# A third buffer for x, one mask tile, and a new order of VectorE's work in a routing attention followed by an MLP

## The chip, the cores and the metric

The kernel runs on one core of one Trainium2 chip. The metric is the device time of one execution in microseconds, as the median of a few runs. The core has five engines with a queue of instructions each, and each queue runs in order: TensorE (PE in the profile, its weight loads PEld), VectorE (DVE), ScalarE (ACT), GpSimd (POOL) and SyncE (SP). Engines wait for each other through semaphores. All transfers between DRAM and SBUF run on 16 shared DMA engines. In this kernel SyncE issues most of them, and GpSimd the small ones and those that add to their target.

## The reference

There are two parts. The first is attention over 4 batches, 8 heads, 768 positions and a head size of 64, in which a query sees only the keys that were routed to the same one of 16 clusters. The second is an MLP with a layer norm and a residual on the 512 features of the joined heads.

```python
q_assign = argmax(q_n @ c_n.T)            # q_n, k_n, c_n: rows over their norms
k_assign = argmax(k_n @ c_n.T)
mask = q_assign[:, None] == k_assign[None, :]
scores = where(mask, q @ k.T / sqrt(D), -1e9)
attn = exp(scores - max) / (sum(exp(scores - max)) + 1e-9)
x = (attn @ v), heads side by side        # (4, 768, 512)
xn = (x - mean) / sqrt(var + 1e-6) * g_ln
out = x + relu(xn @ w_ch1) @ w_ch2        # 512 -> 2048 -> 512
```

The weights of the MLP come as float64 and are turned to float32 on the chip.

## The kernel before

**Pairs and slots.** The attention handles two heads at a time. There are 16 such pairs n (batch and head pair), and each is worked in two slots, one for each half of the 768 queries. A slot has six steps, one for each block of 128 keys. A step i is `scores(i)` and later `weigh(i)`.

- `scores` (L390) makes a 128 x 768 block of scores in PSUM: two matmuls that add the mask and two of keys by queries (L406). ScalarE then takes the exponential into a tile e (L401; eight buffers). PSUM has three buffers for scores, so TensorE can be three steps ahead of ScalarE.
- `weigh` (L411) multiplies e with v into the accumulator a_ps (L418). On VectorE it adds the six e tiles of a slot to a running sum es for the denominators (L432, L435). After the last step ScalarE copies the accumulator into the pair's x tile (L444). x has two buffers, `xs[n]` (L439).

**Preparing the next pair.** For pair n + 1, k is turned (`prep_transpose`, L273), on VectorE in 32 x 32 blocks when it was loaded in the layout for that (`blocks`, L78; line 280). q is turned in that way for pair 1 and from pair 7 on, and on TensorE with a copy by ScalarE for pairs 2 to 6 (L285, L290). `prep_sims` (L305, matmul L312) makes the similarities to the centroids, `prep_turn` (L324) turns them, and `prep_route` (L333) finds the best cluster and writes one-hots on VectorE (L337, L339). `prep_onehot` (L349) turns the one-hots, and ScalarE shades them into two tiles, m and mask, which are the mask's factors (L375). There are two of each.

**Finishing a pair.** `finish(n, part)` (L448) has four parts. Part 0 sums es over the keys by a matmul (den_ps, L455), copies it (L463) and sends the rows to DRAM and back in another layout (flat, rdens: L465, L466). Part 1 takes reciprocals on VectorE (L470), sends them to DRAM (row, L472) and loads them broadcast over the partitions into rb (L480, one buffer). Part 2 multiplies x with rb in place of rb (L487) and stores it. This frees the x buffer. Part 3 turns the product into y (L496) and stores that too. Parts 2 and 3 of pair n run two pairs later.

**Other work between.** For the MLP, weights are converted in chunks: six VectorE instructions (`split_weight`, `join_weight`, L245 to L265) and a transfer by GpSimd that adds to the target (L268). That is two chunks a pair up to pair 6 and one afterwards (`convert`, L622). The layer norm of the first batch (`norm_rows`, `norm_stats`, `norm_stat_rows`, `norm_apply`), sums of its x (`x_sum`) and of the first weights (`w1_sums`) are hung onto pairs 6 to 15 by `put` (L598).

**What sets the order.** The attention is in two blocks `manual_schedule` (L628, L666). Inside a block TensorE, VectorE and ScalarE take instructions in the order in which the program lists them. SyncE's order in the second block is set by a scheduler that builds the program, and so is how the two blocks interlock at their seam, which lies between the first three steps' scores with the turning of k and q of pair 1, and the loop over the slots. In the loop (L667) a slot of pair n lists, before the change: its scores; in slot 0 `finish(n - 1, 0)` and the similarities of n + 1; in slot 1 the one-hots and masks of n + 1; then the conversion; then the weighing with VectorE's sums; then in slot 0 `finish(n - 2, 2)` and `(.., 3)`, the turning of the similarities and the routing of n + 1, and in slot 1 `finish(n - 1, 1)` and the turning of k and q of n + 2; last, the jobs that `put` has hung there. VectorE's part of that, for slot 0 of a middle pair:

```
conversion (6), sums (5), scaling L487, turning y L496, best L337, one-hots L339
```

and for slot 1:

```
conversion (6), sums (5), reciprocals L470, turning k (and q) L280
```

**After the attention** come two layers for each of the four batches, both as Strassen-like products of seven with sums on VectorE and ScalarE (`first_layer`, L791; `second_layer`, L879). The first batch's layers need nothing of the last pair, but the matmul of the last denominators (`finish(15, 0)`, L925) stands ahead of it in TensorE's order.

Of the kernel before, what the change touches and what calls it, by code (L numbers as in the profile page):

```python
# [8 lines left out]
F32 = mybir.dt.float32  # L9
BF16 = mybir.dt.bfloat16  # L10
# [9 lines left out]
def kernel(  # L20
# [11 lines left out]
    nc = tc.nc  # L32
    B, H, S, D = q.shape
    NCL = centroids.shape[1]
    DM, FF = moe_w_ch1.shape
    P = 128
# [19 lines left out]
    def pool(name, bufs, **kw):  # L56
        return stage.enter_context(tc.tile_pool(name=name, bufs=bufs, **kw))

    loads = pool("loads", 1)
    heads = pool("heads", 2)  # L60
# [4 lines left out]
    last = pool("last", 1)  # L65
# [4 lines left out]
    def ps(name, dt=F32, n=512):  # L70
        return pools["t"].tile([P, n], dt, tag="t", name=name)

    pairs = [(b, pr) for b in range(B) for pr in range(NPAIR)]
# [4 lines left out]
    blocks = {  # L78
        (n, name) for n in range(1, len(pairs)) for name in ("qk" if n == 1 or n >= TWICE else "k")
    }  # L80
# [63 lines left out]

    mask = [heads.tile([P, S], BF16, name=f"mask_{i}", bufs=1) for i in range(2)]
    for m in mask:
        nc.gpsimd.memset(m, 0.0)
    hits = const.tile([P, B * NPAIR], F32, name="hits")  # L150
    far = const.tile([P, 2], F32, name="far")
    for rows, bias, scale in ((slice(0, D), 0.0, 1.0), (slice(D, P), -FAR, FAR)):
# [118 lines left out]
    prepared = {n: {} for n in range(len(pairs))}  # L271

    def prep_transpose(n, side, halves=range(NHALF)):  # L273
        src = loaded[n]["qk"[side]]
        if 0 in halves:
            prepared[n][side] = heads.tile([P, S], F32, tag=f"t{side}", name=f"t{side}")
        t_sb = prepared[n][side]
        if (n, "qk"[side]) in blocks:
            if 0 in halves:
                nc.vector.transpose(t_sb, src)  # L280
            return
        if n:
            t = ps_s.tile([P, 2, 512], F32, tag="s", name="qk_ps")
            for c in range(NT):
                nc.tensor.transpose(  # L285
                    t[:, c // TH, c % TH * P : (c % TH + 1) * P],
                    src[:, c, :, :].rearrange("p h d -> p (h d)"),
                    ident,
                )
            nc.scalar.copy(t_sb.rearrange("p (g c) -> p g c", g=NHALF), t[:, :, :HC])  # L290
            return
        for g in halves:
            t = ps_s.tile([P, 2, 512], F32, tag="s", name="qk_ps")[:, 0]
            for c in range(TH):
                nc.tensor.transpose(
                    t[:, c * P : (c + 1) * P],
                    src[:, g * TH + c, :, :].rearrange("p h d -> p (h d)"),
                    ident,
                )
            if side == 0 or g == 1:  # L300
                nc.scalar.copy(t_sb[:, g * HC : (g + 1) * HC], t[:, :HC])
            else:
                nc.vector.tensor_copy(t_sb[:, g * HC : (g + 1) * HC], t[:, :HC])
# [45 lines left out]
    def prep_onehot(n):  # L349
        t = ps("oh_ps", BF16, 1024)  # L350
        for g in range(NHALF):
            for c in range(TH):
                o = (g * TH + c) * P
                nc.tensor.transpose(
                    t[:, o : o + P],
                    onehot[:, c, g, :, :, :].rearrange("p s j d -> p (s j d)"),
                    identb,
                )

        m = heads.tile([P, S], BF16, tag="m", name="m")  # L360
        shade(n, m, t[:, :S], slice(0, P))
        z = mask[n % 2]
        prepared[n]["oh"] = t
        prepared[n]["m"] = [(z[:D], m[:D]), (m[D:], z[D:])]

    def prep_mask(n, j):
        t, z = prepared[n]["oh"], mask[n % 2]
        src, dst = ((D, 0), (Q, D + Q))[j]
        src, dst = slice(src, src + NCL), slice(dst, dst + NCL)
        shade(n, z[dst], t[src, :S], src)  # L370

    def shade(n, out, src, rows):
        add, factor = far[rows, 0:1], far[rows, 1:2]
        if n:
            nc.scalar.activation(out, src, AF.Identity, bias=add, scale=factor)  # L375
        else:
            nc.vector.tensor_scalar(out, src, factor, add, op0=ALU.mult, op1=ALU.add)  # L377
# [6 lines left out]
    xs = {}  # L384
# [26 lines left out]
    def weigh(i):  # L411
        n, g, c = steps[i]
        e = soft[i]
        if c == 0:
            accs[n, g] = ps_a.tile([P, 512], F32, tag="a", name="a_ps")
        acc = accs[n, g]
        for j in range(2):
            nc.tensor.matmul(  # L418
                acc[j * D : (j + 1) * D, :HC],
                loaded[n]["v"][:, j, c, :],  # L420
                e[:, j, :],
                start=(c == 0),
                stop=(c == NT - 1),
            )

        if c == 1:
            if n + 1 < len(pairs):
                es = last.tile([P, 2, HC], F32, tag="es", name="es", bufs=3)
            else:
                es = xpool.tile([P, 2, HC], F32, tag="row", name="es", bufs=2)  # L430
            sums[n, g] = es
            nc.vector.tensor_tensor(es, soft.pop(i - 1), soft.pop(i), ALU.add)  # L432
        elif c > 1:
            es = sums[n, g]
            nc.vector.tensor_tensor(es, es, soft.pop(i), ALU.add)  # L435
        if c == NT - 1:
            if g == 0:
                if n + 1 < len(pairs):
                    xs[n] = last.tile([P, S], F32, tag="x", name="x", bufs=2)  # L439
                else:  # L440

                    late["all"] = xpool.tile([P, 3, S], F32, tag="sums", name="late", bufs=2)
                    xs[n] = late["all"][:, 0]
            nc.scalar.copy(xs[n][:, g * HC : (g + 1) * HC], accs.pop((n, g))[:, :HC])  # L444
# [153 lines left out]
    def put(n, slot, f, *args):  # L598
        extra.setdefault((n, slot), []).append(lambda: f(*args))
# [1 line left out]
    put(6, 0, norm_load, 0)  # L601
    put(6, 1, rows_load, 0, 0)
    for t in range(NT):
        put(7 + t // 2, t % 2, norm_rows, 0, t)
    put(9, 1, norm_stats, 0)
    put(10, "between", norm_stat_rows, 0)
    for i in range(2):
        for c in range(NDC):
            put(10 + 2 * i + c // 2, 1 if i == 0 else c % 2, norm_apply, 0, i, c)
    put(14, 0, x_sum, 0, 1)  # L610
    put(14, 1, x_sum, 0, 2)
    put(15, 1, w1_sums, 0, 0, (0, 1))

# [50 lines left out]
    with tc.manual_schedule(engines=order | {mybir.EngineType.Pool}):  # L666
        for u in range(len(pairs) * slots):  # L667
            n, slot = divmod(u, slots)
            nxt = n + 1 < len(pairs)
            own = range(GROUP * u, GROUP * (u + 1))  # L670
            if slot == 0 and not nxt:
                finish(n - 1, 0)
            for i in own:
                if i >= AHEAD:
                    scores(i)
            if slot == 0:
                if n and nxt:
                    finish(n - 1, 0)
                if nxt:
                    prep_sims(n + 1)  # L680
            elif nxt:
                prep_onehot(n + 1)
                prep_mask(n + 1, 0)
                prep_mask(n + 1, 1)
                if n + 2 < len(pairs) and (n + 2, "q") not in blocks:
                    prep_transpose(n + 2, 0)
                    load(n + 3, "q")
            for job in extra.pop((n, "between"), ()) if slot else ():
                job()
            if (n, slot) in convert:  # L690
                m = convert[n, slot]
                split_weight(m)
                join_weight(m)
                load_weight(m + 1)
            for i in own:
                weigh(i)
            if slot == 0:
                load(n + 1, "v")
                if n > 1:
                    finish(n - 2, 2)  # L700
                    finish(n - 2, 3)
                if nxt:
                    prep_turn(n + 1)
                    prep_route(n + 1)
                else:
                    finish(n - 1, 1)
            elif not nxt:
                for part in (2, 3):
                    finish(n - 1, part)
            else:  # L710
                if n:
                    finish(n - 1, 1)
                if n + 2 < len(pairs):
                    for side in (1, 0):
                        if (n + 2, "qk"[side]) in blocks:
                            prep_transpose(n + 2, side)
                            load(n + 3, "qk"[side])
            for job in extra.pop((n, slot), ()):
                job()

# [471 lines left out]
```

## Time and profile before

The time is 952.88 us, the median of three runs (950.92 to 953.88). The profiled execution spans 951.0 us.

| engine | busy us | share | instructions |
|---|---|---|---|
| TensorE | 922.8 | 97% | 4664 |
| VectorE | 618.1 | 65% | 1106 |
| ScalarE | 346.7 | 36% | 549 |
| GpSimd | 79.2 | 8% | 147 |

By stage, from the busy time in windows, in us and as the share of DMA engines in use:

| window | TensorE | VectorE | ScalarE | DMA |
|---|---|---|---|---|
| 60 to 100 | 38.3 of 40 | 35.2 | 26.2 | 0.88 |
| 100 to 150 | 45.2 of 50 | 42.2 | 30.6 | 0.83 |
| 150 to 200 | 48.8 of 50 | 46.8 | 32.1 | 0.93 |
| 200 to 250 | 48.2 of 50 | 45.0 | 38.0 | 0.84 |
| 250 to 300 | 42.4 of 50 | 38.2 | 27.6 | 0.72 |
| 300 to 350 | 49.4 of 50 | 45.8 | 36.2 | 0.52 |
| 600 to 700 | 100.0 of 100 | 45.5 | 16.3 | 0.11 |

A line of a timeline reads: start in us, duration in us (of the group, if several are merged), engine, line of the kernel, operation, output <- inputs, shape, count, and in brackets how long the engine was idle before it and what ended that wait. In a line of groups the two numbers after the bar are busy us in all and mean ns of one. The attention ends at about 364 us, with the last denominators' matmul; after that the two layers run.

### The profile page before, as it was taken

The page shows a single profiled execution, that of the slowest core. Times are in us where ns is not written, and L with a number is a line of the kernel's source. Part 1 is how long each engine was busy: PE and PEld are TensorE (multiplying, and loading weights), DVE is VectorE, ACT ScalarE, POOL GpSimd, SP SyncE. Part 2 cuts the span into 40 slices and gives each one's busy share as a digit, 9 for nine tenths or more (in the row PEclk, how much of TensorE's full clock was granted, in tenths as well). Part 3 has the DMA queues.
Part 4 walks back from the last instruction along what each step waited for, and adds up shares of the span by engine and source line. Part 5 has one row for each costly group of instructions (what it writes and reads, how often), then busy time and mean ns, then how long its engine had stood idle before and what let it go on. Part 6 is the DMA issues. An engine that isn't in the chain of part 4 may idle for free.

```text
span 951.0 us, 12611 instructions
## 1 busy us (share of the span) xinstructions
PE 922.8 (97%) x4664; PEld 591.0 (62%) x4664; DVE 618.1 (65%) x1106; ACT 346.7 (36%) x549; POOL 79.2 (8%) x147
## 2 busy tenths in 40 slices
PE   8999989999969999999999999999999999999997
PEld 5444444444434445557887557887557887556886
DVE  5998889999599987798882446362436472344431
ACT  4776657677647663332001332001332000332000
POOL 2111112121111121110000000000000000000000
PEclk9999999999979999999999999999999999999999
DMA  7668888988758644564451002021002021000011
GB/s 152 155 153 190 189 181 177 203 179 179 158 117 153 154 94 117 137 140 141 136 158 39 0 1 78 22 95 40 1 0 69 32 84 50 1 1 6 29 45 36
DMA packets 179780, 92.48 MB, mean 97 GB/s; under 512 B 145792, under 2 KB 162288, under 8 KB 179712
## 3 DMA queue, kind: packets, MB, share of 16 engines
q1 hardware_dynamic: 170368, 76.20, 33.0%
q0 software_dynamic: 7744, 15.02, 7.8%
q8 instruction: 38, 0.62, 0.3%
q10 hardware_dynamic: 1600, 0.39, 0.2%
q14 instruction: 30, 0.25, 0.1%
HBM read 64.10 MB, written 19.10 MB: 87 GB/s over the span
## 4 chain that ended last, share of the span: by engine, by line
PE 81%; DVE 9%; DMA 5%; issue 2%; ACT 1%; SPq 1%; POOL 0%; DVEq 0%; ACTq 0%; POOLq 0%
PE x_ps L853 17%; PE x_ps L760 16%; PE s_ps L406 10%; PE z_ps L853 9%; PE a_ps L418 8%; PE z_ps L760 8%; PE y_ps L853 4%; PE y_ps L760 4%; DVE es L435 2%; DMA rb<-row 1%; DMA v_sb<-in_v_dram 1%; DMA row<-rdens 1%; DVE w L260 1%; DVE tb L265 1%; DVE ta L248 1%
## 5 line engine op out<-in xcount | busy, mean ns | idle before, releaser
L406 PE MATMUL s_ps<-t,t 64*128 64x384 f32 x768 | 158.8, 492 | 0.0
L401 ACT ACTIVATE e<-s_ps 128x768 f32<-128x768 f32 x192 | 150.7, 814 | 21.6 <-PE s_ps L406 20.7
L435 DVE TENSOR_TENSOR es<-es,e 128x768 f32<-128x768 f32 x128 | 122.7, 958 | 14.7 <-ACT e L401 1.7
L418 PE MATMUL a_ps<-e,v_sb 128*64 128x384 f32 x768 | 130.9, 490 | 0.0
L780 DVE TENSOR_TENSOR h<-z_ps,u 128x384 f32<-128x384 f32 x64 | 35.6, 556 | 94.0 <-PE z_ps L760 71.9
L418 PEld LDWEIGHTS a_ps<-e,v_sb 128*64 128x64 f32 x768 | 52.3, 137 | 70.0 <-issue 58.1
L406 PEld LDWEIGHTS s_ps<-t,t 64*128 64x128 f32 x768 | 69.9, 191 | 33.8 <-issue 32.9
L853 PE MATMUL x_ps<-w2t,h 128*128 128x256 f32 x384 | 84.5, 379 | 0.0
L788 ACT ACTIVATE h<-h 128x384 f32<-128x384 f32 x96 | 49.6, 522 | 87.5 <-DVE h L780 87.5
L406 PE MATMUL s_ps<-m,mask 64*128 64x384 bf16 x192 | 63.0, 329 | 17.6 <-ACT e L401 17.6
L853 PEld LDWEIGHTS x_ps<-w2t,h 128*128 128x128 f32 x384 | 72.7, 190 | 10.1
L406 PE MATMUL s_ps<-mask,m 64*128 64x384 bf16 x192 | 63.0, 330 | 0.4 <-DVE mask L377 0.4
L775 ACT COPY u<-x_ps 128x384 f32<-128x384 f32 x64 | 30.6, 478 | 78.1 <-PE x_ps L760 78.1
L864 DVE TENSOR_TENSOR o_sb<-x_ps,xb 128x256 f32<-128x256 f32 x48 | 20.2, 420 | 50.2 <-PE x_ps L853 50.2
L775 ACT COPY p<-x_ps 128x384 f32<-128x384 f32 x32 | 14.9, 467 | 98.0 <-PE x_ps L760 98.0
L760 PE MATMUL x_ps<-xt,ws 128*128 128x384 f32 x128 | 46.6, 487 | 0.8 <-DVE ws L593 0.8
L444 ACT COPY x<-a_ps 128x384 f32<-128x384 f32 x30 | 14.3, 478 | 89.9 <-DVE rb L487 63.6
L760 PE MATMUL x_ps<-xn,w 128*128 128x384 f32 x128 | 46.6, 487 | 0.0
L760 PE MATMUL x_ps<-xt,w 128*128 128x384 f32 x128 | 46.5, 486 | 0.0
L760 PE MATMUL y_ps<-xn,w 128*128 128x384 f32 x128 | 46.5, 486 | 0.0
L760 PE MATMUL z_ps<-xn,ws 128*128 128x384 f32 x128 | 46.5, 486 | 0.0
L760 PE MATMUL z_ps<-xt,ws 128*128 128x384 f32 x128 | 46.5, 486 | 0.0
(146 smaller groups left out, 1382.9 us busy)
## 6 DMA issues: line engine op xcount, KB each, us to landing
raw<-in_moe_w_ch_dram SPq DMA_DIRECT2D x32, 512.0 KB, 4.5
w<-tb POOLq DMA_DIRECT2D x32, 256.0 KB, 5.1
v_sb<-in_v_dram SPq DMA_DIRECT2D x32, 192.0 KB, 4.6
xn<-xT_d SPq DMA_DIRECT2D x16, 384.0 KB, 5.3
xr<-x_d SPq DMA_DIRECT2D x24, 256.0 KB, 2.9
xb<-x_d SPq DMA_DIRECT2D x48, 128.0 KB, 2.2
out_dram<-o_sb SPq DMA_DIRECT2D x48, 128.0 KB, 1.7
k_sb<-in_k_dram SPq DMA_DIRECT2D x62, 96.0 KB, 3.9
```

Of the source, the lines that this page charges most:

```text
L248: nc.vector.scalar_tensor_tensor(out=ta, in0=hi, scalar=0xC0000000, in1=ta, op0=ALU.bitwise_and, op1=ALU.bitwise_or)
L401: nc.scalar.activation(e, s[:, :, :HC], AF.Exp, scale=SCALE)
L406: nc.tensor.matmul(s[:, j, :HC], of_keys[:, keys], of_queries[:, cols], start=part == first, stop=part != first, skip_group_check=True,)
L418: nc.tensor.matmul(acc[j * D : (j + 1) * D, :HC], loaded[n]["v"][:, j, c, :], e[:, j, :], start=(c == 0), stop=(c == NT - 1),)
L435: nc.vector.tensor_tensor(es, es, soft.pop(i), ALU.add)
L444: nc.scalar.copy(xs[n][:, g * HC : (g + 1) * HC], accs.pop((n, g))[:, :HC])
L760: nc.tensor.matmul(bank[:, :HC], lhs[:, c, :], rhs[:, c, :], start=first and c == 0, stop=c == NDH - 1, skip_group_check=True,)
L775: nc.scalar.copy(t, bank[:, :HC])
L780: nc.vector.tensor_tensor(h, bank[:, :HC], other, ALU.add)
L788: nc.scalar.activation(h, h, AF.Relu)
L853: nc.tensor.matmul(bank[:, :MH], hidden[lhs + (c,)][:, tt * P : (tt + 1) * P], rhs[:, c, :], start=first and c == 0, stop=c == NFH - 1, sk ...
L864: nc.vector.tensor_tensor(o, bank[:, :MH], x, ALU.add)
```

## The change

x gets a third buffer. The scaling and the turning of y (parts 2 and 3 of pair n - 2) move from slot 0, behind the sums, to slot 1, ahead of the sums. The third buffer is what makes that possible, since x of a pair now lives longer; the move is meant to take the copy of a_ps out of the wait for the scaling. The turning of k and q for the next pair moves from the end of slot 1 to the head of the next slot 0, so that it is done one slot before its use, not two. The conversion of weights moves behind the sums of its slot, so that the sums come as soon as the exponentials are there. The rows of the layer norm, its two passes of `norm_apply` and the sums of x and w1 are hung onto later places, so that the rows of statistics that come back from DRAM have more time to land. m and the mask go down to one tile each, which makes room in SBUF for the third x.

VectorE's work is now, for slot 0 and slot 1 of a middle pair:

```
turning k (and q), sums, conversion, best, one-hots
scaling, turning y, sums, conversion, reciprocals
```

In the order of the built program TensorE and ScalarE have the same sequences as before. VectorE's first sums (pair 0, slot 0) now stand ahead of the turning of k and q of pair 1, which is written in the first block; before, they stood behind it.

```diff
--- before.py
+++ after.py
@@ -144,9 +144,8 @@
-    mask = [heads.tile([P, S], BF16, name=f"mask_{i}", bufs=1) for i in range(2)]
-    for m in mask:
-        nc.gpsimd.memset(m, 0.0)
+    mask = heads.tile([P, S], BF16, name="mask", bufs=1)
+    nc.gpsimd.memset(mask, 0.0)
     hits = const.tile([P, B * NPAIR], F32, name="hits")
     far = const.tile([P, 2], F32, name="far")
     for rows, bias, scale in ((slice(0, D), 0.0, 1.0), (slice(D, P), -FAR, FAR)):
@@ -357,14 +356,14 @@
                     identb,
                 )
-        m = heads.tile([P, S], BF16, tag="m", name="m")
+        m = heads.tile([P, S], BF16, tag="m", name="m", bufs=1)
         shade(n, m, t[:, :S], slice(0, P))
-        z = mask[n % 2]
+        z = mask
         prepared[n]["oh"] = t
         prepared[n]["m"] = [(z[:D], m[:D]), (m[D:], z[D:])]
     def prep_mask(n, j):
-        t, z = prepared[n]["oh"], mask[n % 2]
+        t, z = prepared[n]["oh"], mask
         src, dst = ((D, 0), (Q, D + Q))[j]
         src, dst = slice(src, src + NCL), slice(dst, dst + NCL)
         shade(n, z[dst], t[src, :S], src)
@@ -436,7 +435,7 @@
         if c == NT - 1:
             if g == 0:
                 if n + 1 < len(pairs):
-                    xs[n] = last.tile([P, S], F32, tag="x", name="x", bufs=2)
+                    xs[n] = last.tile([P, S], F32, tag="x", name="x", bufs=3)
                 else:
                     late["all"] = xpool.tile([P, 3, S], F32, tag="sums", name="late", bufs=2)
@@ -601,15 +600,15 @@
     put(6, 0, norm_load, 0)
     put(6, 1, rows_load, 0, 0)
     for t in range(NT):
-        put(7 + t // 2, t % 2, norm_rows, 0, t)
+        put(7 + t // 2, 1, norm_rows, 0, t)
     put(9, 1, norm_stats, 0)
     put(10, "between", norm_stat_rows, 0)
     for i in range(2):
         for c in range(NDC):
-            put(10 + 2 * i + c // 2, 1 if i == 0 else c % 2, norm_apply, 0, i, c)
-    put(14, 0, x_sum, 0, 1)
-    put(14, 1, x_sum, 0, 2)
-    put(15, 1, w1_sums, 0, 0, (0, 1))
+            put(11 + 2 * i + c // 2, 1, norm_apply, 0, i, c)
+    put(15, 0, x_sum, 0, 1)
+    put(15, 0, x_sum, 0, 2)
+    put(15, 0, w1_sums, 0, 0, (0, 1))
@@ -670,6 +669,11 @@
             own = range(GROUP * u, GROUP * (u + 1))
             if slot == 0 and not nxt:
                 finish(n - 1, 0)
+            if slot == 0 and n and nxt:
+                for side in (1, 0):
+                    if (n + 1, "qk"[side]) in blocks:
+                        prep_transpose(n + 1, side)
+                        load(n + 2, "qk"[side])
             for i in own:
                 if i >= AHEAD:
                     scores(i)
@@ -687,22 +691,24 @@
                     load(n + 3, "q")
             for job in extra.pop((n, "between"), ()) if slot else ():
                 job()
+            if slot and n > 1 and nxt:
+                finish(n - 2, 2)
+                finish(n - 2, 3)
+            for i in own:
+                weigh(i)
             if (n, slot) in convert:
                 m = convert[n, slot]
                 split_weight(m)
                 join_weight(m)
                 load_weight(m + 1)
-            for i in own:
-                weigh(i)
             if slot == 0:
                 load(n + 1, "v")
-                if n > 1:
-                    finish(n - 2, 2)
-                    finish(n - 2, 3)
                 if nxt:
                     prep_turn(n + 1)
                     prep_route(n + 1)
                 else:
+                    for part in (2, 3):
+                        finish(n - 2, part)
                     finish(n - 1, 1)
             elif not nxt:
                 for part in (2, 3):
@@ -710,11 +716,6 @@
             else:
                 if n:
                     finish(n - 1, 1)
-                if n + 2 < len(pairs):
-                    for side in (1, 0):
-                        if (n + 2, "qk"[side]) in blocks:
-                            prep_transpose(n + 2, side)
-                            load(n + 3, "qk"[side])
             for job in extra.pop((n, slot), ()):
                 job()
```

## The prediction

> **What bounds the kernel now.** I read the page's list of slices first, then TensorE's timeline with its waits, then the two engines that those waits name. From about 370 us on, TensorE runs the two layers without a gap, and the change moves nothing there. So only the attention part, up to 364 us, can gain or lose. TensorE's waits over 1 us in it, in its timeline:
>
> ```profile
> 91.36 0.32 PE L406 MATMUL s_ps<-m,mask 64*128 64x384 bf16 x1 [1.71 <-ACT e L401]
> ...
> 114.41 0.32 PE L406 MATMUL s_ps<-m,mask 64*128 64x384 bf16 x1 [1.90 <-ACT e L401]
> ...
> 138.47 0.32 PE L406 MATMUL s_ps<-m,mask 64*128 64x384 bf16 x1 [2.91 <-ACT e L401]
> ...
> 182.16 0.32 PE L406 MATMUL s_ps<-m,mask 64*128 64x384 bf16 x1 [1.20 <-ACT e L401]
> ...
> 234.16 0.32 PE L406 MATMUL s_ps<-m,mask 64*128 64x384 bf16 x1 [1.78 <-ACT e L401]
> ...
> 273.23 0.48 PE L406 MATMUL s_ps<-m,mask 64*128 64x384 bf16 x1 [7.57 <-ACT e L401]
> ```
>
> All six name the exponentials. What held ScalarE itself back, in its timeline, at the largest, and what VectorE was doing meanwhile:
>
> ```profile
> 271.98 0.48 ACT L444 COPY x<-a_ps 128x384 f32<-128x384 f32 x1 [12.83 <-DVE rb L487]
> ```
> ```profile
> 260.76 1.83 DVE L556 TENSOR_TENSOR xn<-xn,stat_row 128x768 f32<-128x768 f32 x2 [8.34 <-DMA stat_row<-stat_d]
> ...
> 270.94 0.95 DVE L487 TENSOR_TENSOR rb<-x,rb 128x768 f32<-128x768 f32 x1
> ```
>
> The copy of the weighed sums (L444) wants one of two x buffers; the older is freed by the scaling (L487); VectorE, in order, stood 8.3 us at the norm's first subtraction. The same copy waits before four of the other stalls; only that at 234 us is different (two table loads on ScalarE).
>
> The cost is more than the 15.3 us of those five waits. I compared where the weighing of each pair's second slot starts: 72.13, 94.99, 118.04, 143.13, 163.44, 185.13 ... 248.14, 278.81, 299.12 us. An undisturbed pair takes 20.97 us while q is turned on TensorE (pairs 0 to 4) and 20.31 after. The excess is 1.89, 2.08, 4.78, 1.38 and 10.36: 20.5 us. The other 5.2 us are matmuls at half clock after the long waits (0.48 against 0.32 us each).
>
> **What the Trainium skill says.** "Perfetto Trace Analysis", Optimization Strategy: a gap that repeats on the engine that should be saturated can mean too few buffers for the next tile. The trace agrees: x has two. "TensorE: Matmul & The Clock Gate", What's actually happening: after an idle window of some 3.4 us the clock halves. Here it halves after 2.91 and 7.57 us of idling and not after 1.90. "DMA: Bandwidth & Descriptors", Queues, rings and completion order: an engine consumes one ring's descriptors in ring order. I use this below for two GpSimd transfers issued back to back; the trace of before has them some 5 us apart, so it doesn't show this directly.
>
> **The change part by part.** The built order of TensorE and ScalarE is the same, instruction for instruction. Only VectorE's order and the loads change.
>
> *Third x buffer, scaling a slot later.* The copy no longer has anything to wait for: the scaling it needs lies 20 us back. All 20.5 us are up for removal.
>
> *Norm's apply a pair later.* Its rows (landed at 260.8) are then some 20 us old: the 8.3 us wait goes; already in the 20.5.
>
> *One mask, one m.* The new mask is written after the turning of the one-hots, which stands behind all scores of the old pair in TensorE's order: nothing.
>
> *Start.* The built order puts the first slot's sums ahead of turning k and q of pair 1. Before:
>
> ```profile
> 16.95 0.98 DVE L280 STREAM_TRANSPOSE t<-k_sb 128x768 f32<-128x768 f32 x1 [2.66 <-DMA k_sb<-in_k_dram]
> 17.86 0.94 DVE L280 STREAM_TRANSPOSE t<-q_sb 128x768 f32<-128x768 f32 x1
> ```
> ```profile
> 18.85 0.85 PE L312 MATMUL sim_ps<-t,cT 128*32 128x384 f32 x8 [0.68 <-DVE t L280]
> ```
>
> The sums can begin at 16.3 (exponentials from 14.70, 0.8 apart) and take 5.2 (the row's five start to start), to 21.5; two turnings of 0.9 end at 23.3. TensorE's similarities, with the weighing queued behind, start at 23.35 instead of 18.85: **+4.5**, and the idle stretch of 5.2 us may halve the clock (0 to 2.5; I take **+1.5**).
>
> *End.* Two sums of x (0.9, 0.8) and two of w1 (0.8) now stand before the last slot's sums, and so does the conversion (3.3), which used to run while the slot before was waiting for exponentials. Before, the last two slots' sums started at 347.88 and 356.86, both on exponentials. Now: 347.9 + 5.2 sums + 3.3 + 1.9 scaling and turning + 0.15 + 2.5 = 361.0, + 5.2 = 366.2 against 362.1. The denominators' matmul started at 363.79; it starts at about 366.3: **+2.5**.
>
> *The middle, where the cost is unsure.* VectorE's work for a pair, start to start: sums 5.2 x 2, conversions 3.3 x 2 (one from pair 7), best and one-hot 1.05, scaling and turning y 1.9, reciprocal 0.15, turning k 0.85 (and q 0.85): 20.9 us to pair 5 and 21.8 at pair 6, against TensorE's 20.97 and 20.31. It has no room. Two new waits hang on it:
> (a) turning k and q of the next pair stands at the head of the slot whose similarities need it, 5.6 us after the slot's start (scores 4.9, denominators 0.7). On paper VectorE reaches it at 1.8 and is done at 2.6: 3 us of room, where there was a slot.
> (b) the scaling waits, at the head of VectorE's second slot, for the reciprocals to go to DRAM and come back. This loop is (round trip L) + scaling 1.9 + sums 5.2 + conversion 3.3 + reciprocal 0.15 = L + 10.5. Before, L is seen here:
>
> ```profile
> 95.71 0.86 POOL L268 DMA_DIRECT2D w<-tb x1 [4.51 <-DVE tb L265]
> 100.97 0.57 POOL L472 DMA_DIRECT2D row<-rdens x1 [4.40 <-DVE rdens L470]
> 105.77 1.08 POOL L480 DMA_DIRECT2D rb<-row x2 [4.23 <-DMA row<-rdens]
> ```
> ```profile
> 100.45 0.22 DVE L470 RECIPROCAL rdens<-rdens 128x12 f32<-128x12 f32 x1
> ...
> 112.12 0.96 DVE L487 TENSOR_TENSOR rb<-x,rb 128x768 f32<-128x768 f32 x1 [2.20 <-DMA rb<-row]
> ```
>
> L was 11.7 there, and about 9 after pair 5. In the new order the conversion ends right before the reciprocal, so its 256 KB transfer goes out just ahead of the 6 KB one instead of 5 us ahead. From the page's medians: 5.1 for that transfer, 0.8 more for the small one behind it (an estimate: 1.8 when alone, most of it in parallel), 1.1 issue, 4.5 for the broadcast: L = 11.5. Low end 10 (the queue is empty by then: y's writes come earlier), high end 13.
> With 11.5 the loop is 22.0. VectorE's lag at a slot's head, pair by pair, starting at 1.25 at pair 2, grows to 2.05, 3.1, 4.15, 5.85 at pair 6, where turning k and q ends at 7.5 against 5.6: a stall of 1.9, then 1.7 and 0.1: **+3.7**. From pair 8 the lag stays at some 3.7, as VectorE's 20.2 us a pair hardly recovers it; at pair 9 the square root on ScalarE then waits for the statistics, which come at 23.8 instead of 22.2: **+1.6**. With L = 10 the first is 0; with 13 the same recurrence gives stalls of 1.6, 2.55, 4.1, 3.2, 1.6: 13, and 2.4 for the root.
>
> Sum: 952.9 - 20.5 + 6.0 + 2.5 + 3.7 + 1.6 = 946.2. I say **946.5**.
>
> **The rivals.**
> *Round trip short* (L = 10): 952.9 - 20.5 + 6 + 2.5 + 1.6 = 942.5, and 939 if the clock holds at the start and the root doesn't wait. For it: y's writes are out of the way when the small transfers go. Against: the big one is directly ahead of them.
> *Round trip long* (L = 13): 952.9 - 20.5 + 6 + 2.5 + 15.4 = 956.3: **slower**, the new loop takes all that the buffer gave. For it: VectorE is full and DMA 0.83 to 0.93 busy from 60 to 250 us. Against: it needs transfers slower than their medians in every pair, and TensorE's stalls also relieve DMA.
> *Buffer alone counts*: scheduling costs nothing at start and end: 932 to 935. Against: the order of the built program at the start is plain.
>
> **How the numbers follow.** Forecast (943 to 950) 0.48; short round trip 0.22; long 0.24; buffer alone 0.06. The range takes in the low end of the short case and most of the long one: 939 to 957, with one in ten outside on each side. 0.3% are 2.9 us: faster means under 950.0. Forecast, short case and buffer alone lie there, less a little of the forecast's upper edge: 0.70; of the long case half lies within 0.3%: same 0.15, slower 0.15.
>
> **What would show it.** No wait of the copy of x on the scaling, and none of 7 us near 265. A wait of 5 us on the turned k or q near 18 to 23 us, and one of 3 us on the last sums before the last denominators. Waits of TensorE's similarities on the turning at pairs 5 to 7, with VectorE's scaling waiting 1 us or more for the broadcast at pairs 2 to 7. Pairs 11 to 14 at 20.31 us. I am wrong if the scaling waits 3 us or more in each early pair (the loop), or if TensorE waits on the one-hots or the e buffers, which I give over 3 us of room, or if it stalls nowhere in the middle.

## Result, and the profile after

The changed kernel takes **958.34 us** (median of 4 runs, 956.99 to 959.12); the kernel before, beside it, 953.29 (4 runs, 950.92 to 953.88). The ratio is 1.0056, 95% interval 1.0035 to 1.0077: slower by half a per cent, where the forecast was 946.5. The profiled spans are 951.0 us before and 957.3 after. Line numbers from `mask` to the loop over the slots are one lower than before (L443 is the copy that was L444, L486 the scaling that was L487), and those of the layers behind it one higher.

TensorE's timeline of the changed kernel, its longer waits in the attention part (start, duration, instruction, and in brackets the idle time ahead of it and what ended it):

```profile
23.18 1.51 PE L311 MATMUL sim_ps<-t,cT 128*32 128x384 f32 x8 [5.10 <-DVE t L279]
...
134.67 0.84 PE L311 MATMUL sim_ps<-t,cT 128*32 128x384 f32 x4 [2.33 <-DVE t L279]
...
157.11 0.85 PE L311 MATMUL sim_ps<-t,cT 128*32 128x384 f32 x8 [1.96 <-DVE t L279]
...
204.39 1.51 PE L311 MATMUL sim_ps<-t,cT 128*32 128x384 f32 x8 [4.31 <-DVE t L279]
...
247.46 0.47 PE L405 MATMUL s_ps<-m,mask 64*128 64x384 bf16 x1 [3.06 <-ACT e L400]
...
370.53 0.85 PE L454 MATMUL den_ps<-es,ones 128*32 128x384 f32 x6 [1.55 <-DVE es L434]
```

Of the six old waits only the square root's is left, and it has grown (1.78 to 3.06). The four above it are new and all name one thing: the turned k and q (L279) come late from VectorE.

A wait is not its cost (half clock follows some of them, and a pair may catch up), so I read the cost as the prediction did, from the starts of each pair's second weighing. Each figure is the time from the pair ahead, less the undisturbed 20.97 us (up to pair 4) or 20.31 (after):

| us | pair 0 starts at | 3 | 4 | 5 | 6 | 7 | 8 | 10 | 11 | span |
|---|---|---|---|---|---|---|---|---|---|---|
| before | 30.18 | 1.89 | 2.08 | 4.78 | 0 | 1.38 | 0 | 2.07 | 10.36 | 951.0 |
| after | 37.07 | 0 | 0.91 | 3.14 | 3.84 | 0.46 | 6.90 | 4.76 | 0 | 957.3 |

From these: the five stalls -20.5; the start 37.07 - 30.18 = +6.9; pairs 4 to 7 +8.35; pair 8 +6.9; the square root 4.76 - 2.07 = +2.7; the stretch after pair 15's weighing (957.3 - 363.48 against 951.0 - 359.12) +1.9. The sum is +6.3, which is the difference of the spans. (A column has the number of the pair at which the step ends: "3" is from pair 2 to pair 3. Columns left out are 0 in both, but for pair 15's, which is -0.94 and -0.93.)

Three places in VectorE's timeline stand behind it. The start, where the first slot's sums are now ahead of the turning:

```profile
16.17 0.96 DVE L431 TENSOR_TENSOR es<-e 128x768 f32<-128x768 f32 x1 [1.95 <-ACT e L400]
17.23 4.15 DVE L434 TENSOR_TENSOR es<-es,e 128x768 f32<-128x768 f32 x4
21.30 0.97 DVE L279 STREAM_TRANSPOSE t<-k_sb 128x768 f32<-128x768 f32 x1
22.19 0.94 DVE L279 STREAM_TRANSPOSE t<-q_sb 128x768 f32<-128x768 f32 x1
```

The round trip of the reciprocals, on GpSimd's timeline (transfers are issued there) and then on VectorE's:

```profile
109.83 0.86 POOL L267 DMA_DIRECT2D w<-tb  x1 [7.79 <-DVE rdens L469]
110.38 0.88 POOL L471 DMA_DIRECT2D row<-rdens  x1
116.68 1.08 POOL L479 DMA_DIRECT2D rb<-row  x2 [5.42 <-DMA k_sb<-in_k_dram]
```
```profile
109.44 0.22 DVE L469 RECIPROCAL rdens<-rdens 128x12 f32<-128x12 f32 x1
...
123.26 0.96 DVE L486 TENSOR_TENSOR rb<-x,rb 128x768 f32<-128x768 f32 x1 [3.28 <-DMA rb<-row]
```

The converted weights' 256 KB (L267) go out directly ahead of the 6 KB row (L471); the broadcast (L479), which needs the row, is issued 6.3 us after it; over six pairs 5.4 to 6.4, mean 5.9. Before, with 5.2 us between weights and row, this took 2.1 to 5.7. From the reciprocal's start to the scaling's are 13.8 us here; over the six pairs 12.7, 13.1, 13.8, 11.3, 12.2 and 12.9, mean 12.7. The scaling itself stands 0.76 to 3.28 us in them.

And pair 8, where the second of two norm rows stands ahead of the turning, in VectorE's timeline and in that of SyncE's queue:

```profile
201.59 0.69 DVE L526 BATCH_NORM_STATS2 bn<-xr 128x6 f32<-128x512 f32 x1 [3.08 <-DMA xr<-x_d]
202.32 0.18 DVE L527 BATCH_NORM_AGGREGATE mv<-bn 128x2 f32<-128x6 f32 x1
202.50 0.98 DVE L279 STREAM_TRANSPOSE t<-k_sb 128x768 f32<-128x768 f32 x1
```
```profile
192.54 4.88 SPq L498 DMA_DIRECT2D x_d<-y  x4
197.46 1.20 SPq L518 DMA_DIRECT2D xr<-x_d  x2
```

The second row's load is listed only where the first row is taken (`rows_load(b, t + 1)` in `norm_rows`); one row to a slot gave that load half a pair. Here SyncE's queue first issues the four stores of y, which takes 4.9 us; the second row's load leaves at 197.46, only 0.2 us before VectorE takes the first row (197.66). VectorE stands 3.08 us, and TensorE behind it 4.31.

### The profile page after: what moved, and what is told of

Read it like the earlier page. It is cut to its first block, busy times and chain, and to the rows that moved or that the text cites. A ratio compares the mean times of both kernels' runs of the same rounds, so it can differ in the third digit from the quotient of the medians.

```text
span 957.3 us, 12594 instructions
## 1 busy us (share of the span) xinstructions
PE 928.3 (97%) x4664; PEld 590.2 (62%) x4664; DVE 618.7 (65%) x1106; ACT 349.4 (36%) x549; POOL 77.9 (8%) x146
## 4 chain that ended last, share of the span: by engine, by line
PE 82%; DVE 9%; DMA 4%; issue 3%; ACT 2%; SPq 1%; POOL 0%; ACTq 0%; DVEq 0%; POOLq 0%
PE x_ps L854 17%; PE x_ps L761 16%; PE s_ps L405 11%; PE a_ps L417 9%; PE z_ps L854 9%; PE z_ps L761 8%; PE y_ps L854 4%; PE y_ps L761 4%; DVE es L434 2%; DMA k_sb<-in_k_dram 1%; PE sim_ps L311 1%; DMA rb<-row 1%; PE den_ps L454 1%; ACT e L400 1%; DVE w L259 1%
## 5 line engine op out<-in xcount | busy, mean ns | idle before, releaser
L400 ACT ACTIVATE e<-s_ps 128x768 f32<-128x768 f32 x192 | 152.7, 811 | 28.1 <-PE s_ps L405 25.9
L405 PE MATMUL s_ps<-t,t 64*128 64x384 f32 x768 | 156.3, 486 | 0.0
L417 PE MATMUL a_ps<-e,v_sb 128*64 128x384 f32 x768 | 136.3, 506 | 0.0
L776 ACT COPY p<-x_ps 128x384 f32<-128x384 f32 x32 | 14.9, 467 | 97.9 <-PE x_ps L761 97.9
L761 PE MATMUL x_ps<-xn,ws 128*128 128x384 f32 x128 | 46.5, 486 | 0.0
```

The source lines that it names most:

```text
L400: nc.scalar.activation(e, s[:, :, :HC], AF.Exp, scale=SCALE)
L405: nc.tensor.matmul(s[:, j, :HC], of_keys[:, keys], of_queries[:, cols], start=part == first, stop=part != first, skip_group_check=True,)
L417: nc.tensor.matmul(acc[j * D : (j + 1) * D, :HC], loaded[n]["v"][:, j, c, :], e[:, j, :], start=(c == 0), stop=(c == NT - 1),)
L761: nc.tensor.matmul(bank[:, :HC], lhs[:, c, :], rhs[:, c, :], start=first and c == 0, stop=c == NDH - 1, skip_group_check=True,)
L776: nc.scalar.copy(t, bank[:, :HC])
```

## Experiments

Twelve kernels. Ratios are to the kernel before, run beside each, with 95% intervals; "excess" is the reading of the table above.

### Mending one cost at a time, and all three

Turning of pair 1 at the head of the second block of the schedule:

```
-        for side in (1, 0):
-            prep_transpose(1, side)
-            load(2, "qk"[side])
     with tc.manual_schedule(engines=order | {mybir.EngineType.Pool}):
+        for side in (1, 0):
+            prep_transpose(1, side)
+            load(2, "qk"[side])
```

> The changed kernel, but the turning of k and q of pair 1 is listed at the head of the second block, so that VectorE does it before the first sums. Theory: the first sums ahead of it cost 6.9 us (weighing of slot 1 of pair 0 at 37.07 us against 30.18 before), and all later work is only shifted; so about 951.5 us, and that weighing back at about 30.2. Rival: k of pair 1 isn't there until about 17 us anyway and VectorE, which is full, gives the time back further on; then 956 to 958.

Measured: 950.55 us (20 runs), ratio 0.998 (0.9968 to 0.9992). The weighing of pair 0 starts at 29.40 again (37.07 in the changed kernel). All other waits stay: 2.80 at 127.43, 1.56 at 171.43, 4.75 at 196.67, 3.24 at 240.45, 1.56 at 363.72. The order of two instruction groups at the start costs its 7 us all the way to the end.

Norm rows one to a slot as before:

```
-        put(7 + t // 2, 1, norm_rows, 0, t)
+        put(7 + t // 2, t % 2, norm_rows, 0, t)
```

> The changed kernel, with the norm's rows one per slot as in the kernel before, not two in slot 1. Theory: the second row of pair 7's two comes late from DRAM (VectorE waits 3.1 us for xr at 201.6), which holds the turning of k and q behind it and TensorE's similarities for 4.3 us and then halves the clock; 6.9 us in all at pair 8, so about 951.5 us. Rival: VectorE is late there because it is full and has carried a lag from the pairs before; then the wait only moves to another instruction and 956 to 958 stay.

Measured: 952.52 us (12 runs), ratio 0.9999 (0.9983 to 1.0015). Pair 8's excess falls from 6.90 to 1.50, pair 10's from 4.76 to 3.36. The start stays (pair 0 at 37.31).

The reciprocal ahead of the conversion in slot 1:

```
             for i in own:
                 weigh(i)
+            if slot and n and nxt:
+                finish(n - 1, 1)
             if (n, slot) in convert:
...
-            else:
-                if n:
-                    finish(n - 1, 1)
```

> The changed kernel, with the reciprocals and their transfers ahead of slot 1's conversion instead of behind it. Theory: the loop of round trip, scaling, sums, conversion and reciprocals (12.6 + 10.5 = 23.1 us against 20.3 to 21.0 of TensorE) makes the stalls of pairs 4 to 7 (8.4 us); with the conversion out of the loop and its 256 KB transfer behind the small one the loop is below 19 us and these stalls go: about 950 us, no wait of the similarities before pair 8. Rival: VectorE's work a pair (20.9 to 21.8 us) is what is too long; it is the same here, so the same stalls: 957 to 959.

Measured: 952.38 us (12 runs), ratio 0.9994 (0.9976 to 1.0013). The row now goes out before the weights: issued at 101.92, broadcast at 105.36, 3.4 us (2.4 to 5.2 over the six pairs, mean 3.4). The scaling waits nowhere in pairs 2 to 7, and the excess of pairs 4 to 7 is 1.6 instead of 8.35. Part of that is lost again at the square root, where the excess of pair 10 rises from 4.76 to 7.57. Not a single instruction of VectorE was taken out. That speaks against the rival "VectorE is simply full": what filled it was the wait.

All three:

> The three edits of the other kernels of this call together. Theory: their gains add, 958.3 - 6.9 - 6.9 - 8.4 = 936, with the wait around the square root at pair 9 and 10 (4.8 us, of which 2.1 were there before) and the end left. Rival (VectorE full): with the slots before no longer stretched by stalls, VectorE falls behind and new waits take the place of those removed: 945 or more.

Measured: 939.92 us (4 runs), ratio 0.9873 (0.9831 to 0.9916). Taken from the changed kernel's 958.34, the three alone gain 7.8, 5.8 and 6.0, a sum of 19.6; all together they gain 18.4. They nearly add up, so they are mostly separate costs. It misses the 936 by 4 us; the trace (span 936.1) still has the square root's wait, 3.07 at 227.60, the tail's 1.56, and an excess of 2.8 in pairs 6 to 8.

### Parts of the change on the kernel before

The third buffer by itself, with one mask and one m:

```
-                    xs[n] = last.tile([P, S], F32, tag="x", name="x", bufs=2)
+                    xs[n] = last.tile([P, S], F32, tag="x", name="x", bufs=3)
```

> The kernel before with only the third buffer for x, and one mask and one m to make room for it; every operation stays in its old place, so the scaling still stands in slot 0. Theory (the copy of the weighed sums waited for a buffer alone, and nothing else of the change was needed): the 20.5 us of the five stalls go, so 932 to 936 us, and TensorE shows no wait of over 1 us in pairs 2 to 7. Rival (VectorE is what is late: its scaling still waits for the broadcast ahead of the routing, and the wait moves on to the masks or the similarities): 945 to 952 us, with TensorE waiting on those instead.

Measured: 951.05 us (20 runs), ratio 0.9996 (0.9984 to 1.0009): nothing. My theory fell. The copies of x wait no more, but the excesses sum to 22.5, as before (22.6). VectorE and then TensorE, in their timelines:

```profile
136.46 0.96 DVE L486 TENSOR_TENSOR rb<-x,rb 128x768 f32<-128x768 f32 x1 [3.67 <-DMA rb<-row]
...
138.91 0.56 DVE L338 SCALAR_TENSOR_TENSOR onehot<-simT_ps,best 128x384 bf16<-128x384 f32 x1
```
```profile
139.53 0.51 PE L353 MATMUL oh_ps<-identb,onehot 128*128 128x128 bf16 x6 [3.46 <-DVE onehot L338]
```

The scaling waits 3.67 us for the broadcast, the one-hots of the next pair are queued behind it, and TensorE now waits for those. The buffer that the copy waited for was the last link; the cause was that VectorE stands in a DMA's round trip ahead of the routing. The Trainium skill ("Perfetto Trace Analysis", Optimization Strategy) reads a repeating gap as possibly too few buffers; here the added buffer moved the gap and did not shorten it.

The same with the norm's subtraction and scaling a pair later (`put(11 + 2 * i + c // 2, 1, norm_apply, ...)`, and the first `x_sum` in slot 1):

> As the buffer alone, and the norm's subtraction and scaling a pair later (with x_sum a slot later, since it reads what these write). Theory (the third buffer takes away the stall of pair 11 as well, whatever VectorE waits for): the same time as the buffer alone, within 2 us. Rival (at pair 11 VectorE stands waiting for the broadcast rows of mean and deviation for over 7 us, and a buffer doesn't help that): 5 to 10 us less than the buffer alone.

Measured: 945.27 us (10 runs), ratio 0.993 (0.991 to 0.9949): 5.8 us less than the buffer alone, so the rival holds. Pairs 11 and 12 lose 4.44 and 2.53 us with the buffer alone and nothing here. A buffer does not help an engine that stands waiting for rows that have not landed: with the buffer alone VectorE still stands 6.47 us at the norm's subtraction.

And with the scaling in slot 1, behind the conversion:

```
+            if slot and n > 1 and nxt:
+                finish(n - 2, 2)
+                finish(n - 2, 3)
             for i in own:
                 weigh(i)
             if slot == 0:
                 load(n + 1, "v")
-                if n > 1:
-                    finish(n - 2, 2)
-                    finish(n - 2, 3)
```

> The kernel before with the third buffer, one mask and one m, the scaling in slot 1 behind the conversion and ahead of the sums, and the norm's subtraction and scaling a pair later (x_sum a slot later, since it reads what these write). Conversions stay ahead of the sums, k and q are turned behind slot 1, and norm rows come one to a slot as before. Theory (the stalls before came from VectorE standing at the scaling for the broadcast ahead of the routing, and all the rest of the change only costs): 20 us under the kernel before, 931 to 936 us; between the reciprocal and the scaling lie 14.6 us of other VectorE work, more than the 11.7 of the round trip, so the scaling waits under 0.5 us. Rival (the turning at a slot's head and the conversions behind the sums were needed): 943 us or more, with TensorE waiting on the turning or the sums.

Measured: 942.72 us (4 runs), ratio 0.99 (0.9879 to 0.9921). The mechanism is as the theory has it: the scaling waits in no pair up to 14, and the excess of pairs 3 to 5 is gone. The size is not: 942.7 and not 936, next to the rival's 943, and the rival's sign is there too, small: TensorE waits 1.49 us for the sums and twice 0.98 for the turning. Pairs 6 and 7 have a new excess of 1.5 and 5.0, with VectorE waiting 2.09 us for raw weights at 156.23, and the square root costs 3.2. Whether the weights' loads are the whole of it was not tried.

### Where k and q are turned

The changed kernel with the turning behind slot 1 as before (two pairs ahead):

> The changed kernel with the turning of k and q put back behind slot 1, two pairs ahead. Theory (the turning at a slot's head is the door through which every delay of VectorE reaches TensorE: the start 6.9 us, pair 8 6.9 us, pairs 4 to 7 8.35 us): 939 to 944 us, with no wait of a similarity on the turning; the scaling's waits for the broadcast stay. Rival (the loop over the denominators delays TensorE by another way, through the sums and the denominators): the start and pair 8 come back alone or less, 945 to 952 us.

Measured: 973.06 us (4 runs), ratio 1.0213 (1.0171 to 1.0255), 15 us *slower* than the changed kernel. Both theories fell. The start's wait, which the theory had put down to the turning's place, stays at 5.10. The queue that issues the loads, and VectorE:

```profile
195.77 2.69 SPq L86 DMA_DIRECT2D k_sb<-in_k_dram  x4
198.59 4.40 SPq L86 DMA_DIRECT2D q_sb<-in_q_dram  x4
203.34 2.10 SPq L518 DMA_DIRECT2D xr<-x_d  x2
```
```profile
206.94 0.69 DVE L526 BATCH_NORM_STATS2 bn<-xr 128x6 f32<-128x512 f32 x1 [9.55 <-DMA xr<-x_d]
```

With the turning ahead of the norm's rows, the loads of k and q are issued ahead of the row's, 7.6 us of issuing, and the second row of the slot comes 9.55 us late instead of 3.08; at pair 10 the wait is 8.66 and the square root stands behind it (TensorE 11.82). To test that, the same with one row to a slot:

> The changed kernel with k and q turned behind slot 1, and norm rows one to a slot as before. Theory (the turning behind slot 1 was slow only since the second row of a slot waited 9.55 us for a load that the same queue sends behind those of k and q): the 20 us of pairs 8 and 11 go; the start's 6.9 us stay; 943 to 950 us. Rival (the turning behind slot 1 is itself what delays TensorE): 960 us or more.

Measured: 958.15 us (4 runs, 954.27 to 959.54), ratio 1.0062 (1.004 to 1.0085). The one row to a slot gives back 14.9 us, most of the 20 that the theory had; the rest it misses, and the rival's 960 is not reached either. TensorE still waits for the turning four times in pairs 5 to 8 (1.24, 1.65, 1.30, 0.98) and 5.82 us at the square root. So the turning's place is no lever for the waits of pairs 5 to 8. VectorE's order says why: turning "behind slot 1" and "at the next slot's head" differ only by the norm's rows that lie between. But the place is not free: with the same rows and the turning at the slot's head (norm rows one to a slot, 952.52) the kernel is 5.6 us faster. In the traces it is pair 10 that differs (7.46 here, 3.36 there): the two turnings now stand ahead of the last norm row, and ScalarE waits 4.05 us for the statistics where it waited 1.30. The profiled run was this kernel's shortest, so its trace explains the lower edge of these times and not all of the median.

### One edit: the conversions

The changed kernel, conversions back ahead of the sums, all else as changed:

```
+            if (n, slot) in convert:
+                m = convert[n, slot]
+                split_weight(m)
+                join_weight(m)
+                load_weight(m + 1)
             for i in own:
                 weigh(i)
-            if (n, slot) in convert:
-                m = convert[n, slot]
-                split_weight(m)
-                join_weight(m)
-                load_weight(m + 1)
```

> The changed kernel with the conversions back ahead of the sums, all else kept (turning of k and q at a slot's head, two norm rows to a slot, the late sums). In its built order the turning of k and q of pair 1 stands ahead of the sums again. Theory (the conversions behind the sums make the start's 6.9 us, and the long round trip with its 8.35 us in pairs 4 to 7): 940 to 944 us, with no start wait, the scaling's wait for the broadcast under 0.5 us, and pair 8's wait still there. Rival (the loop is as long with the conversion elsewhere, since the same work lies in it): the start alone comes back, 949 to 952 us.

Measured: **943.33 us** (4 runs), ratio 0.9908 (0.9886 to 0.993), 15.0 us under the changed kernel by moving the six VectorE instructions of each conversion, and with them their transfers. The start is back (pair 0 at 30.04; the built order has the turning of pair 1 ahead of the sums), pairs 4 to 7 fall from 8.35 to 4.4, pair 8 from 6.90 to 0.42, the tail by 2.3. Only the square root is dearer (7.0). The round trip, GpSimd and then VectorE:

```profile
95.65 0.86 POOL L267 DMA_DIRECT2D w<-tb  x1 [6.60 <-DVE tb L264]
100.90 0.57 POOL L471 DMA_DIRECT2D row<-rdens  x1 [4.40 <-DVE rdens L469]
103.47 1.17 POOL L479 DMA_DIRECT2D rb<-row  x2 [1.99 <-DMA row<-rdens]
```
```profile
100.39 0.22 DVE L469 RECIPROCAL rdens<-rdens 128x12 f32<-128x12 f32 x1
...
112.03 0.95 DVE L486 TENSOR_TENSOR rb<-x,rb 128x768 f32<-128x768 f32 x1
```

The weights leave 5.2 us ahead of the row, the broadcast follows the row by 2.6 us (2.0 to 3.4 over the pairs), and the scaling (no bracket) waits for nothing. The rival, a loop just as long, would have shown a wait there. Of what is left in pairs 4 to 7 VectorE's waits for raw weights may be the cause (1.27, 0.47 and 0.63 us); that was not tried.

One thing was not expected: pair 8's wait is gone, though two norm rows still share a slot. SyncE's queue:

```profile
180.72 2.61 SPq L498 DMA_DIRECT2D x_d<-y  x4
183.37 3.47 SPq L518 DMA_DIRECT2D xr<-x_d  x2
```

The stores of y take 2.6 us of issuing here, not 4.9, and the second row's load leaves 3.2 us before VectorE comes to that row (186.61, no wait). With only the reciprocal moved ahead of the conversion the stores take 4.6 us, and the row's wait stays, 3.51. So pair 8's 6.9 us take both: two rows to a slot, and a queue that is slow ahead of the second row's load. Why the stores leave faster here was not tried. At the square root the second row still waits here, 2.23 us.

### Tail, and a best version

All three mends, and `x_sum` at the end of pair 14, `w1_sums` behind pair 15's sums:

> All three mends, and besides x_sum at the end of pair 14 and w1_sums behind pair 15's last sums, so that 2.8 us of VectorE no longer stand ahead of the last sums. Theory (the tail's wait of 1.56 us is VectorE's order): 938 us, 1.5 to 2 us under the three mends, with no wait of TensorE for the last sums. Rival (the gain is eaten in pair 14 or by the first matmuls of the expert layer, which need x_sum and w1_sums): 940 us, no difference.

Measured: 939.78 us (4 runs), ratio 0.987 (0.9831 to 0.9909), the same as without. The wait for the last sums is gone, and matmuls at the start of the MLP wait instead, in TensorE's timeline and then VectorE's:

```profile
350.86 1.53 PE L760 MATMUL x_ps<-xt,ws 128*128 128x384 f32 x4 [2.65 <-DVE ws L592]
```
```profile
347.98 0.96 DVE L486 TENSOR_TENSOR rb<-x,rb 128x768 f32<-128x768 f32 x1 [3.72 <-DMA rb<-row]
...
349.87 0.38 DVE L592 TENSOR_TENSOR ws<-w 128x256 f32<-128x256 f32 x1
```

The rival holds: `w1_sums` (L592) now stands behind the last scaling, and that waits 3.72 us for its broadcast. It is the same round trip once more.

The changed kernel with the conversions ahead, one row to a slot and the square root a slot later:

```
-    put(9, 1, norm_stats, 0)
+    put(10, 0, norm_stats, 0)
```

> The changed kernel with three mends: conversions ahead of the sums, norm rows one to a slot, and the square root of the statistics a slot later (end of pair 10's slot 0). Theory (in the changed kernel with only the conversions ahead, TensorE's one long wait left is 5.36 us at the square root, since ScalarE holds there for the statistics, which hold for the second row of the slot): ScalarE no longer waits between its two table loads, TensorE's wait shrinks to the 1.8 us that the kernel before had there, and its half clock after it goes: 937 to 939 us, under the 939.9 of the three mends of the earlier runs. Rival (the two table loads alone cost it, or the later square root moves the wait to the rows of mean and deviation, with VectorE waiting for them at pair 11): 941 us or more.

Measured: **938.01 us** (5 runs, 936.67 to 938.62), ratio 0.9838 (0.9807 to 0.9869), below both kernels, and as the theory had it. ScalarE's timeline at the square root, and then TensorE's wait:

```profile
237.56 1.28 ACT L533 ACT_TABLE_LOAD   x1
238.85 0.30 ACT L533 ACTIVATE stat<-mv,eps 128x6 f32<-128x6 f32 x1
239.17 1.28 ACT L400 ACT_TABLE_LOAD   x1
```
```profile
241.32 0.32 PE L405 MATMUL s_ps<-m,mask 64*128 64x384 bf16 x1 [1.31 <-ACT e L400]
```

No wait stands between the two table loads any more, and the excess of pair 10 is 1.6. Both edits have a part in that: ScalarE stood 3.58 us between the loads with the conversions ahead alone, 1.30 with the three mends, where the rows are one to a slot and the square root is in its old place, and not at all here. What is left is an excess of 2.0 to 2.4 in each of pairs 5 to 7. Whether this beats the three mends (939.92, measured beside other runs) the intervals do not tell.

## Why the prediction was wrong, step by step

- **"All 20.5 us are up for removal"**: right for the changed kernel, where all five stalls are gone. The reason given ("the copy no longer has anything to wait for") was the last link only: the buffer alone brought nothing, and the later scaling and the norm's later apply are what it takes. Put on the kernel before, these bring 10 us, for VectorE has other waits in the middle. Read net by pair, pairs 3 to 7 lost 10.13 us before and lose 8.35 now, to a VectorE that still stands for the broadcast; most of what was gained is pair 11's 10.36, where the norm's apply comes later.
- **Start, +6.0**: right, +6.9. The wait is 5.10 us, as predicted, and the weighing of the first slot at half clock takes 5.99 us instead of 4.09. "The built order" puts it there because of the conversions: with these ahead of the sums it is gone.
- **(b), L = 11.5, +3.7: right in kind, mis-sized.** L is 12.7 and pairs 4 to 7 cost 8.35, between the 3.7 worked out for 11.5 and the 13 for 13. Of its terms the row behind the weights came out (5.1 + 0.8 = 5.9, measured mean 5.9), and the broadcast nearly (1.1 + 4.5 = 5.6, measured 5.8). Left out was what lies ahead of the row: 0.94 us from the reciprocal's start to the row's issue (109.44 to 110.38), in which GpSimd issues the weights; 0.52 of it is there in the kernel before too. By the prediction's own two figures a microsecond of L is worth some 6 us, so this microsecond is enough for the difference (an estimate from 3.7 at 11.5 and 13 at 13). The page of the Trainium skill that it drew on ("DMA: Bandwidth & Descriptors", Queues, rings and completion order) says of the queues of SyncE and ScalarE that descriptors are consumed in ring order; for GpSimd's the runs show only the times, 5.9 us directly behind the weights and 2.6 with the weights 5.2 us ahead and the conversions ahead of the sums.
- **(a), "3 us of room, where there was a slot": wrong.** There had been no slot: in VectorE's order the turning already stood at the slot's head, behind the reciprocal. So it does not now come "one slot before its use, not two"; it stands where it stood. What the change put between the slot's sums and the turning are the conversion and the norm's rows, and ahead of the sums the scaling that waits.
- **Norm's rows two to a slot, not costed at all: the step that failed.** The prediction goes through buffer, apply, masks, start, end and the two waits of the middle, and leaves out this edit: the rows' own time on VectorE fits into its 20.2 us a pair, a wait for them is in no term. Taking it back gives 5.8 us, since the second row's load is issued only with the first row's use, behind what the same queue already holds. It costs that much only where the queue is slow ahead of that load: with the conversions ahead of the sums pair 8 loses 0.42 with the same two rows. With pair 8's 6.9 the sum would have been 953, no change.
- **Square root, +1.6**: +2.7; one row to a slot takes 1.4 of it back.
- **End, +2.5**: +1.9, with a wait of 1.55 and not 3 us. With the conversions ahead it is gone, though the sums of x and w1 stay late.
- **Pairs 11 to 14 at 20.31**: right. **"One mask, one m: nothing"**: right, TensorE's waits of 0.9 us and more name them in no run.

Measured less forecast, these terms are +6.9 for pair 8, +4.65 for (b), +0.9 for the start, +1.1 for the root and -0.6 for the end: 13 us, from 6.7 faster to 6.3 slower.

Of the rivals, the long round trip (956.3) came nearest, in part for another reason: it had 13 us for the loop and 2.4 for the root, where 8.35 and 2.7 were measured; pair 8 is the rest. That its total lies 2 us from the measured one is luck.

## What to carry to other kernels

When a wait names a buffer, follow it to the engine that should have freed it, and ask what that engine was waiting for: if it stands in a DMA's round trip, another buffer moves the wait to whatever else is queued behind, and moving the instruction away from the round trip shortens it. Moving a block of work from ahead to behind another on an in-order engine moves its transfers too; look at what then leaves directly ahead of a small transfer that somebody waits for. And cost every edit of a diff, the one-word ones too: a load that is issued by its predecessor's use has just the time between two uses.

## What the runs showed of the hardware

- A row of 6 KB directly behind 256 KB in GpSimd's queue: 5.4 to 6.4 us from its issue to that of the broadcast that needs it, in all six pairs. With the 256 KB 5.2 us earlier: 2.0 to 3.4 with the conversions ahead, but 4.8 to 5.7 in three of six early pairs of the kernel before. What else slows the row there was not tried.
- In the changed kernel TensorE ran at half clock after waits of 5.10 and 4.31 us (eight similarities take 1.51 us then, else 0.85; the weighing behind them 5.99 and 5.84, else 4.09), and not after 2.33. But with the scaling in slot 1 on the kernel before, it did so after two waits of only 1.49 and 0.98 us with 0.85 us of matmuls between, and at the square root a wait of 3.06 us in the changed kernel slowed the next matmul (0.47 us against 0.32) where waits of 3.07 did not in three runs (norm rows one to a slot, the three mends, these with the early x_sum). The Trainium skill ("TensorE: Matmul & The Clock Gate", What's actually happening) has an idle window of some 3.4 us that runs freely and does not start with a wait; in these runs no length of a single wait divides the cases, and half clock came after waits shorter than that window (after 2.80 us in the run with pair 1 turned first: four similarities take 1.31 us, the weighing 5.26).
- At pair 8 a wait of 3.08 us on VectorE stands behind 6.9 us on TensorE: 4.31 of waiting, 0.7 in the similarities, 1.75 in the weighing. With one row to a slot VectorE waits 1.14 there and TensorE loses 1.5.
